# MLP and output projections as pairs of 64-row products, with ScalarE writes at the change of rows

## The chip, the cores and the metric

The kernel runs on one core of one Trainium2 chip. The metric is the time of one execution on the device, in microseconds. TensorE does the matrix products (PE in the profile; its weight loads are PEld), VectorE (DVE) and ScalarE (ACT) the elementwise work, GpSimd (POOL) products of the attention, and SyncE (SP) issues the DMAs.

## The reference

Everything is float32, with x of 2048 rows and D = 448 columns, F = 1792 hidden columns, 16 heads of 28.

```python
x = A_x
g = sigmoid((x * gate_w).sum(-1, keepdims=True))
qkv = x @ wqkv                       # q, k, v of 16 heads
# sliding window: each position attends to 8 positions, 2 apart
idx = pos[:, None] - (arange(8) * 2)[None, :]
attn = softmax(where(idx >= 0, einsum("bhsd,bhswd->bhsw", q, kg) * scale, -1e9))
a = concat_heads(einsum("bhsw,bhswd->bhsd", attn, vg)) @ wo
h = relu(x @ w1 + b1) ** 2
b = h @ w2 + b2
out = g * a + (1 - g) * b
```

## The kernel before

**Three products for one.** Each float32 operand is split into a high part, rounded to the format that TensorE takes (float32r), and a low part, the rest. A product is then high x high, high x low and low x high. ScalarE writes the high part, VectorE subtracts to get the low part (`split_full`, L108).

**The 64 odd rows.** D = 448 is three blocks of 128 rows and 64 rows. For the MLP and the output projection the odd rows are doubled: a tile of w1 holds the low part in rows 0 to 63 and the high part in rows 64 to 127 (`w17`, `split_w7`, L112), and x holds its high part twice (`x7`) and its low part twice (`x8`). Two full-row products do the work of the odd rows. `pairs` (L141) lists the nine products of the three blocks and these two: 11 for one hidden tile or one projection tile.

**Pairs in the qkv stage.** The first stage (q, k, v of four chunks of 512 rows, `qkv_first`, `qkv_two`) already works in pairs: `side_by_side` (L183) issues one product on rows 0 to 63 and one on rows 64 to 127, for two different psum tiles, so that both halves of the array work at once. A psum tile is fed by one half of the rows at a time. To change halves, `turn` (L194) lets VectorE (or, for two tiles, ScalarE) write an unused element of the psum tile; the following products wait for that write.

**The MLP.** The main loop (L821) goes through the four chunks of x in `ORDER` and the 14 tiles f of 128 hidden columns. `mlp_h` (L648) computes a hidden tile (128 x 512) with 11 products in psum bank set "m" (four buffers). `mlp_act` (L657) gives ScalarE three instructions: relu with bias in psum, the square rounded into `hh`, the square in psum; VectorE later subtracts the low part `hl`. `mlp_o` (L707) multiplies hidden tile f with w2 into four psum tiles of set "b" (128 x 448 each, one for 128 rows of x), 12 products for one f, two tiles f behind `mlp_h`. After the last f, `fin_add` (L693) has VectorE scale and add, and the result goes to DRAM.

**Attention and output projection.** GpSimd forms the products of attention beside all this (`qk_piece`, `av_piece`), VectorE reduces them. Finished rows go to DRAM and come back transposed (`wo_load`, L724), are split (`wo_split`, L742: a copy in psum, high parts by ScalarE, low parts by VectorE) and multiplied with wo (`wo_mm`, L757: 11 products for a tile of 128 rows). `wo_step` (L771) places one such tile between two hidden tiles.

**Order.** The order of the instructions on each engine is fixed when the kernel is built, by a clock of planned costs: `advance(dt)` moves it on after each group of matmuls (`MM512`, `MM448` are the planned times of one step), and runs what was put off with `at(dt, fn)`; the attention is a generator that is called by the same clock. The engines then run their queues in order, and wait for each other by semaphores.

Of the kernel before, what the change touches and what calls it, by code (L numbers as in the profile page):

```python
# [38 lines left out]
HL_DELAY = 1700.0  # L39
# [4 lines left out]
LAND_DELAY = 5000.0  # L44
KEY_DELAY = 8000.0
DEFER = 2
ORDER = (3, 0, 1, 2)
RING = 5
# [4 lines left out]
BT_BUFS = 9  # L53
# [3 lines left out]
def gated_mix_kernel(ctx: ExitStack, tc: tile.TileContext, xT, wqkv, w1, w2, wo, b1, b2, out):  # L57
# [23 lines left out]
    w17 = const.tile([P, F], F32R, name="w17")  # L81
# [3 lines left out]
    b1t = const.tile([P, 64], F32, name="b1t")[:, :NF]  # L85
    b2t = const.tile([P, D], F32, name="b2t")
    ident = const.tile([P, P], F32, name="ident")
# [4 lines left out]
    const.tile([P, 64], F32, name="pad_x")  # L92
# [6 lines left out]
    make_identity(nc, ident)  # L99
# [11 lines left out]

    def split_w7(raw, w7, soon=now):  # L112

        nc.scalar.activation(w7, raw, AF.Copy)
        soon(lambda: nc.vector.tensor_sub(w7[0:64], raw[0:64], f32(w7[0:64])))
# [24 lines left out]

    def pairs(xh, xl, x7, x8, wh, wl, w7):  # L141

        r = []
        for k in range(3):
            r += [(xh(k), wh(k)), (xh(k), wl(k)), (xl(k), wh(k))]
        r += [(x7, w7), (x8, w7)]
        return r
# [29 lines left out]
    class Acc:  # L177


        def __init__(self, tag, name, n):  # L180
            self.pt, self.n, self.todo, self.rows = ps(tag, name), n, 21, None

    def side_by_side(*todo):  # L183


        assert len(todo[0]) == len(todo[1])
        for pair in zip(*todo):
            for r, (acc, a, w) in enumerate(pair):
                rows = slice(r * 64, r * 64 + 64)
                assert acc.rows in (None, r)  # L190
                nc.tensor.matmul(acc.pt[:, :acc.n], a[rows], w[rows], start=acc.todo == 21, stop=acc.todo == 1)  # L191
                acc.todo, acc.rows = acc.todo - 1, r

    def turn(one, two):  # L194


        for acc in (one, two) if one is not two else (one,):
            if one is two:
                nc.scalar.activation(acc.pt[0:1, 511:512], ident[0:1, 1:2], AF.Copy)
            else:  # L200
                nc.vector.memset(acc.pt[0:1, 511:512], 0.0)
            acc.rows = None
# [113 lines left out]
    wo_q = []  # L316

# [32 lines left out]
    def o_store(par, s):  # L350
        nc.sync.dma_start(o_d[par, s], o_t.pop((par, s)))
        at(WO_DELAY, lambda: wo_q.append((par, s)))
# [132 lines left out]
    def w1_piece(i, dt):  # L485
# [6 lines left out]
        def part(k):  # L492
            if k < 3:
                split_full(raw[:, k, :n], w1h[:, k, sl], w1l[:, k, sl], soon)
            else:
                split_w7(raw[:, 3, :n], w17[:, sl], soon)
# [120 lines left out]
    hp = ctx.enter_context(tc.tile_pool(name="hidden", bufs=3, reuse_waits="tile"))  # L617
# [6 lines left out]
    wo7 = bw.tile([P, D], F32R, name="wo7")  # L624
# [11 lines left out]
    def x_reload(i, j):  # L636

        c = ORDER[i]
        r = (4 * i + j) % RING
        xt = (xpool if r < 4 else bw).tile([P, 2, CH], F32R, tag=f"x{r}", name=f"x{c}b_{j}")  # L640
        nc.sync.dma_start(f32(xt), x_d[c, j])
        return xt

    hs = {}
    nxt = [x_reload(1, j) for j in range(RING - 4)]
    bw.tile([P, 48], F32, name="pad_b")

    def mlp_h(x, c, f):  # L648
        pt = ps("m", f"h{c}_{f}")
        fs = slice(f * P, f * P + P)  # L650
        pr = pairs(lambda k: x.h[k], lambda k: x.l[k], x.x7, x.x8,
                   lambda k: w1h[:, k, fs], lambda k: w1l[:, k, fs], w17[:, fs])
        for i, (a, w) in enumerate(pr):
            nc.tensor.matmul(pt, w, a, start=i == 0, stop=i == len(pr) - 1)  # L654
        return pt

    def mlp_act(pt, c, f):  # L657
# [5 lines left out]
        at(HL_DELAY, lambda: nc.vector.tensor_sub(hl, pt, f32(hh)))  # L663
# [15 lines left out]

    def fin_ahead():  # L680

        for par, t, *_ in wo_cur + [w[1:] for w in wo_in]:
            fin_fetch(par, t)
# [23 lines left out]
    def mlp_o(c, *fs):  # L707
        ops = [(f, *hs.pop((c, f)), *w2hl(f)) for f in fs]
        last = fs[-1] == NF - 1
        if last:  # L710
            bts = [fin_tile(c // 2, (c % 2) * 4 + tl) for tl in range(4)]
        for tl in range(4):
            if fs[0] == 0:
                bps[tl] = ps("b", f"b{c}_{tl}")
            sl = slice(tl * P, tl * P + P)
            for f, hh, hl, wh, wl in ops:
                for i, (a, w) in enumerate(((hh, wh), (hh, wl), (hl, wh))):
                    nc.tensor.matmul(bps[tl][:, :D], a[:, sl], w, start=f == 0 and i == 0, stop=f == NF - 1 and i == 2)  # L718
        if last:
            for tl in range(4):  # L720
                par, t = c // 2, (c % 2) * 4 + tl
                fin_add(par, t, bts[tl], bps[tl][:, :D], g1t[:, par, t:t + 1])

    def wo_load(par, t):  # L724


        tag = ("ot", "k", "v", "ot")[t // 2] if par else "ot"
        raw = (bp if tag == "ot" else attp).tile([P, 8 * P], F32, tag=tag, name=f"ot{par}_{t}")
        raw = raw.rearrange("p (k t n) -> p k t n", k=4, t=2)
        src = o_d[par, t].rearrange("p c -> (p c)")  # L730

        def rows(m, n):
            return bass.AP(tensor=src.tensor, offset=src.offset + m * 32, ap=[[32, n], [32 * D, 8], [1, 32]])
        rv = raw.rearrange("p k t (q j) -> p k (t q) j", j=32)
        for k in range(3):
            nc.sync.dma_start(rv[:, k], rows(k * P, P))
        for r in range(2):
            nc.sync.dma_start(rv[r * 64:r * 64 + 64, 3], rows(3 * P, 64))
        for i in range(2):
            wo_in.append((clock["pe"] + LAND_DELAY, par, t + i, raw[:, :, i]))  # L740

    def wo_split(par, t, raw):  # L742
        oh = bp.tile([P, 3, P], F32R, tag="oh", name=f"oh{par}_{t}", bufs=2)
        ol = bp.tile([P, 3, P], F32R, tag="ol", name=f"ol{par}_{t}", bufs=2)
        o7 = bp.tile([P, P], F32R, tag="o7", name=f"o7{par}_{t}", bufs=2)
        o8 = bp.tile([P, P], F32R, tag="o8", name=f"o8{par}_{t}", bufs=2)

        pt = ps("m", f"oc{par}_{t}")
        pv = pt.rearrange("p (k n) -> p k n", k=4)
        nc.scalar.activation(oh, raw[:, 0:3], AF.Copy)  # L750
        nc.scalar.activation(pv, raw, AF.Copy)
        nc.scalar.activation(o7, raw[:, 3], AF.Copy)
        nc.vector.tensor_sub(ol, pv[:, 0:3], f32(oh))
        nc.vector.tensor_sub(o8, pv[:, 3], f32(o7))
        return (par, t, oh, ol, o7, o8)

    def wo_mm(st):  # L757
        par, t, oh, ol, o7, o8 = st
        bt = fin_tile(par, t)
        pa = ps("m", f"a{par}_{t}")  # L760
        pr = pairs(lambda k: oh[:, k], lambda k: ol[:, k], o7, o8,
                   lambda k: woh[:, k], lambda k: wol[:, k], wo7)
        for i, (a, w) in enumerate(pr):
            nc.tensor.matmul(pa[:, :D], a, w, start=i == 0, stop=i == len(pr) - 1)  # L764
        fin_add(par, t, bt, pa[:, :D], gt[:, par, t:t + 1])

    wo_loads = [0]
    wo_in = []
    wo_cur = []

    def wo_step():  # L771

        due = len(wo_cur)
        fin_ahead()
        if wo_in and clock["pe"] > wo_in[0][0]:
            wo_cur.append(wo_split(*wo_in.pop(0)[1:]))
            wo_loads[0] -= 1
        while len(wo_q) >= 2:
            (par, t), n = wo_q[0], wo_loads[0]
            if not (n == 0, True, st_["att"] == 1, n <= 4)[t // 2 if par else 0]:  # L780
                break
            del wo_q[:2]
            wo_loads[0] += 2
            at(LOAD_DELAY, lambda par=par, t=t: wo_load(par, t))
        if due:
            wo_mm(wo_cur.pop(0))
# [102 lines left out]
```

## Time and profile before

| | |
|---|---|
| median of 3 runs | 425.2 us (424.85 to 427.08) |
| profiled execution | 424.95 us |
| its span in the trace | 423.2 us |
| TensorE busy | 417.6 us (99%), 2452 matmuls |
| VectorE busy | 273.3 us (65%) |
| ScalarE busy | 185.3 us (44%) |
| GpSimd busy | 272.2 us (64%) |
| qkv stage on TensorE | about 9 to 109 us |
| MLP and projections on TensorE | about 109 to 419 us |
| granted TensorE clock | 0.999 |

How to read the lines below: a timeline row is start, duration (both us), engine, line, operation, out<-in, shapes and count; in square brackets stands the idle time before it and what ended it. A row of the chain in order of time is start, duration and what. A row of groups gives the total busy time and the mean of one instruction in ns. A row of windows gives the length of the stretch, then busy time and instructions of PE, PEld, DVE, ACT and POOL, the granted clock, the DMA share and GB/s. "h" is a hidden psum tile, "b" an MLP output tile, "a" a projection tile, "hh" and "hl" the high and low part of a hidden tile.

### The profile page before, as it was taken

The numbers are of one execution on the slowest core, as the hardware profiler recorded it, in microseconds if no ns is written. First come the engines' busy times: TensorE is split into PE (matmuls) and PEld (weight loads), VectorE is DVE, ScalarE is ACT, GpSimd is POOL, SyncE is SP. The second block draws the span as 40 slices with busy tenths as digits, with TensorE's granted clock in tenths as the row PEclk, the third lists the DMA queues.
The fourth block names the chain that finished last, engine by engine and source line by source line (L and its number), as shares of the span: only waits on it lengthen the run. The fifth ranks groups of instructions, "written<-read, shape, count | busy, mean of one in ns | idle before, by whom it ended". The sixth has DMA issues, their size and how long they took to land.

```text
span 423.2 us, 6516 instructions
## 1 busy us (share of the span) xinstructions
PE 417.6 (99%) x2452; PEld 379.5 (90%) x2452; DVE 273.3 (65%) x400; ACT 185.3 (44%) x372; POOL 272.2 (64%) x167
## 2 busy tenths in 40 slices
PE   8999999999999999999999999999999999999996
PEld 7999999999888888988888888898899888888995
DVE  4520422375499988996575699677577696692463
ACT  3642444344555543543443543534354433344750
POOL 1000000960979999999998989899979699690000
PEclk9999999999999999999999999999999999999999
DMA  7999899939624234551120779185267500237723
GB/s 234 339 338 334 231 376 286 367 102 339 227 68 188 86 137 155 198 207 50 75 83 0 237 265 255 31 237 142 71 159 246 202 24 0 88 125 148 140 87 131
DMA packets 69439, 74.10 MB, mean 175 GB/s; under 512 B 36448, under 2 KB 62496, under 8 KB 69024
## 3 DMA queue, kind: packets, MB, share of 16 engines
q1 hardware_dynamic: 69408, 73.69, 54.1%
q8 instruction: 19, 0.31, 0.3%
q14 instruction: 12, 0.10, 0.1%
HBM read 46.23 MB, written 28.25 MB: 176 GB/s over the span
## 4 chain that ended last, share of the span: by engine, by line
PE 80%; POOL 9%; DVE 6%; issue 2%; DMA 1%; ACT 0%; SPq 0%; DVEq 0%; POOLq 0%
PE h L654 24%; PE b L718 24%; PE qkv L191 23%; PE a L764 8%; POOL av L336 5%; POOL qk L329 4%; DVE w2al L110 1%; DVE wol L110 1%; PE qkv L260 1%; DMA xraw<-xT 1%; DVE o L344 1%; DVE hl L663 1%; DVE bt L694 1%; POOL lg L376 0%; DVE lg L330 0%
## 5 line engine op out<-in xcount | busy, mean ns | idle before, releaser
L329 POOL TENSOR_TENSOR qk<-q,k 128x896 f32<-128x896 f32 x64 | 138.1, 2186 | 93.5 <-DMA k<-k_d 85.6
L336 POOL TENSOR_TENSOR av<-lg,v 128x896 f32<-128x896 f32 x64 | 120.3, 1976 | 8.6 <-DMA v<-v_d 4.0
L660 ACT ACTIVATE h<-h,b1t 128x512 f32<-128x512 f32 x56 | 37.0, 661 | 146.2 <-PE h L654 146.2
L191 PE MATMUL qkv<-wqh,x 64*128 64x448 f32 (+1 forms) x528 | 90.7, 362 | 0.0
L191 PE MATMUL qkv<-wql,x 64*128 64x448 f32 (+1 forms) x264 | 75.3, 361 | 0.0
L191 PEld LDWEIGHTS qkv<-wqh,x 64*128 64x128 f32 x528 | 74.1, 184 | 0.3
L344 DVE TENSOR_REDUCE o<-av 128x112 f32<-128x896 f32 x64 | 66.9, 1066 | 3.9 <-POOL av L336 3.9
L330 DVE TENSOR_REDUCE lg<-qk 128x32 f32<-128x896 f32 x64 | 66.9, 1075 | 3.5 <-POOL qk L329 3.5
L663 DVE TENSOR_TENSOR hl<-h,hh 128x512 fp32r<-128x512 f32 x56 | 38.0, 680 | 33.0 <-ACT h L662 33.0
L210 ACT ACTIVATE st<-qkv 128x448 f32<-128x448 f32 x48 | 24.7, 544 | 48.5 <-PE qkv L191 46.3
L191 PEld LDWEIGHTS qkv<-wql,x 64*128 64x128 f32 x264 | 44.8, 184 | 0.1
L718 PE MATMUL b<-w2ah,hl 128*128 128x448 f32 x112 | 40.7, 364 | 0.3 <-DVE hl L663 0.3
L718 PE MATMUL b<-w2ah,hh 128*128 128x448 f32 x112 | 40.7, 363 | 0.0
L718 PE MATMUL b<-w2bh,hh 128*128 128x448 f32 x112 | 40.6, 363 | 0.0
L718 PE MATMUL b<-w2bh,hl 128*128 128x448 f32 x112 | 40.6, 363 | 0.0
L718 PE MATMUL b<-w2bl,hh 128*128 128x448 f32 x112 | 40.4, 361 | 0.0
L718 PE MATMUL b<-w2al,hh 128*128 128x448 f32 x112 | 40.4, 360 | 0.0
L661 ACT ACTIVATE hh<-h 128x512 fp32r<-128x512 f32 x56 | 33.6, 599 | 1.8
L662 ACT ACTIVATE h<-h 128x512 f32<-128x512 f32 x56 | 33.2, 594 | 0.0
L654 PE MATMUL h<-x1b,w1h 128*128 128x512 f32 x84 | 28.2, 390 | 0.0
L654 PE MATMUL h<-x,w1h 128*128 128x512 f32 x84 | 28.2, 390 | 0.0
L654 PE MATMUL h<-x2b,w1h 128*128 128x512 f32 x84 | 28.2, 389 | 0.0
(105 smaller groups left out, 765.9 us busy)
## 6 DMA issues: line engine op xcount, KB each, us to landing
k<-k_d SPq DMA_DIRECT2D x8, 840.0 KB, 5.1
v<-v_d SPq DMA_DIRECT2D x8, 840.0 KB, 4.6
x_d<-x SPq DMA_DIRECT2D x12, 512.0 KB, 5.1
q_d<-st SPq DMA_DIRECT2D x8, 448.0 KB, 7.7
k_d<-st SPq DMA_DIRECT2D x8, 448.0 KB, 5.0
v_d<-st SPq DMA_DIRECT2D x8, 448.0 KB, 6.3
w1raw<-w SPq DMA_DIRECT2D x4, 896.0 KB, 10.4
q<-q_d SPq DMA_DIRECT2D x8, 448.0 KB, 3.4
```

The costliest lines, as they stand in the source:

```text
L191: nc.tensor.matmul(acc.pt[:, :acc.n], a[rows], w[rows], start=acc.todo == 21, stop=acc.todo == 1)
L329: nc.gpsimd.tensor_mul(pr, q[:, s:s + 1].to_broadcast([P, W, C]), k[:, s:s + W])
L330: pending.append(lambda: nc.vector.tensor_reduce(lg[:, s], pr.rearrange("p w (h d) -> p w h d", h=HG), axis=AX.X, op=ALU.add))
L336: nc.gpsimd.tensor_mul(pr.rearrange("p (h d) w -> p w h d", h=HG), lg[:, s][:, :, :, None].to_broadcast([P, W, HG, DH]), v[:, s:s + W].rea ...
L344: nc.vector.tensor_reduce(o[:, g * C:(g + 1) * C], pr, axis=AX.X, op=ALU.add)
L654: nc.tensor.matmul(pt, w, a, start=i == 0, stop=i == len(pr) - 1)
L660: nc.scalar.activation(pt, pt, AF.Relu, bias=b1t[:, f:f + 1])
L661: nc.scalar.activation(hh, pt, AF.Square)
L662: nc.scalar.activation(pt, pt, AF.Square)
L663: at(HL_DELAY, lambda: nc.vector.tensor_sub(hl, pt, f32(hh)))
L718: nc.tensor.matmul(bps[tl][:, :D], a[:, sl], w, start=f == 0 and i == 0, stop=f == NF - 1 and i == 2)
L764: nc.tensor.matmul(pa[:, :D], a, w, start=i == 0, stop=i == len(pr) - 1)
```

## The change

The MLP's hidden products, its output products and the output projection are all issued as pairs of 64-row products, for two tiles at a time.

- The odd rows get the same three products as the others: `w17` becomes `w17h` and `w17l`, in which the even tiles f lie on rows 0 to 63 and the odd ones on rows 64 to 127; `wo7` becomes `wo7h`, `wo7l`. w1's odd rows are split in more and smaller pieces.
- Two hidden tiles f and f+1 are a couple. `h_first` issues 12 pairs (tile f on the lower half of the rows, f+1 on the upper half, with the odd rows), `h_second` the other 9 with the halves exchanged. Output tiles are taken two and two ("left" 0 and 1, "right" 2 and 3) with 6 pairs before and 6 after the exchange, and projection tiles two and two with 12 and 9.
- Between the halves stands `touch`: ScalarE copies one column of an operand of the last product onto itself (w1h for the hidden tiles, hl for the output tiles, woh for the projection). It waits for the products that read the operand, and the next products that read it wait for it.
- The order of one couple is: `h_first`; the turn of the hidden tiles; first halves of the output products of the couple before; their turn; `h_second`; relu and squares of both tiles; if there is one, the first half of a projection couple; second halves of the output products; the second half of the projection.
- For the second couple of all, the output products and their turns come after `h_second` and its relu and squares; at the end of a chunk the right tiles' first halves and turn do so.
- Projection work starts with the third chunk instead of the second, for two tiles at a time; its low parts are put off by `OL_DELAY`. Two copies into psum per tile become five ScalarE instructions per couple. In the last chunk most projection couples stand at the end.
- Buffers: four hidden buffers for three, eight for nine rows of 448, the identity tile and a pad go, x tiles are reloaded into the slots that the chunk's last products leave first.

```diff
+    def touch(ap):
+        nc.scalar.activation(ap, f32(ap), AF.Copy)
+
+    def go(todo, cost):
+        n = len(todo[0])
+        for a in range(0, n, 3):
+            side_by_side(todo[0][a:a + 3], todo[1][a:a + 3])
+            advance(min(3, n - a) * cost)
+
+    def three(acc, lh, ll, rh, rl):
+        return [(acc, lh, rh), (acc, ll, rh), (acc, lh, rl)]
...
-    def mlp_h(x, c, f):
-        pt = ps("m", f"h{c}_{f}")
...
-        for i, (a, w) in enumerate(pr):
-            nc.tensor.matmul(pt, w, a, start=i == 0, stop=i == len(pr) - 1)
-        return pt
+    def h_first(x, c, f):
+        accs = [Acc("m", f"h{c}_{f + r}", CH) for r in range(2)]
+        go([h_last(x, a, f) + h_full(x, a, f + r, (0, 1, 2)) for r, a in enumerate(accs)], MM512)
+        return accs
+
+    def h_turn(accs, f):
+        touch(w1h[:, 2].rearrange("p (f n) -> p f n", n=P)[:, f:f + 2, 0:1])
+        for a in accs:
+            a.rows = None
+
+    def h_second(x, accs, f):
+        go([h_full(x, accs[1 - r], f + 1 - r, (2, 0, 1)) for r in range(2)], MM512)
...
-        at(HL_DELAY, lambda: nc.vector.tensor_sub(hl, pt, f32(hh)))
+        at(HL_DELAY * (1 + f % 2), lambda: nc.vector.tensor_sub(hl, pt, f32(hh)))
...
+    def o_turn(c, f, tls):
+        hl = hs[c, f + 1][1].rearrange("p (t n) -> p t n", n=P)
+        touch(hl[:, tls[0]:tls[-1] + 1, 0:1])
+        for tl in tls:
+            bps[tl].rows = None
...
+    def wo_first(st):
+        _, _, accs, _, _, o7, o8 = st
+        go([wo_three(accs[r], o7, o8, wo7h, wo7l) + wo_full(st, r, (0, 1, 2)) for r in range(2)], MM448)
+        touch(woh[:, 2, 0:1])
...
+    for g in range(2 * NF):
+        i, f = g // (NF // 2), g % (NF // 2) * 2
+        c = ORDER[i]
+        pc, pf = (c, f - 2) if f else (ORDER[i - 1], NF - 2)
+        ends = f == NF - 2 and i < 3
...
+        accs = h_first(x, c, f)
...
+        h_turn(accs, f)
+        if g > 1:
+            for tls in (left, right)[:1 if ends else 2]:
+                o_part(pc, pf, False, tls)
+            o_turn(pc, pf, left if ends else both)
+        h_second(x, accs, f)
+        for r, acc in enumerate(accs):
+            mlp_act(acc.pt, c, f + r)
...
+        if g == 1:
+            for tls in (left, right):
+                o_part(pc, pf, False, tls)
+                o_turn(pc, pf, tls)
+        elif g > 1 and ends:
+            o_part(pc, pf, False, right)
+            o_turn(pc, pf, right)
+        st = at_hand() if wo_ready or last else None
+        if st:
+            wo_first(st)
...
+        if g:
+            o_all(pc, pf, True)
...
+        if st:
+            wo_second(st)
```

More of the change, by code (lines that the diff above doesn't have):

```diff
@@ L190, in side_by_side @@
                 assert acc.rows in (None, r)
-                nc.tensor.matmul(acc.pt[:, :acc.n], a[rows], w[rows], start=acc.todo == 21, stop=acc.todo == 1)
+                nc.tensor.matmul(acc.pt[:, :acc.n], a[rows], w[rows], start=acc.todo == acc.all, stop=acc.todo == 1)
                 acc.todo, acc.rows = acc.todo - 1, r
@@ L752, in wo_split @@
[L752 to L765, printed above, removed]
```

267 lines of the change are left out of this document (157 added, 110 removed).

## The prediction

> **What bounds the kernel now.** I read the page's totals first, then the chain that ended last, then that chain in order of time.
>
> ```profile
> span 423.2 us, 6516 instructions
> PE 417.6 (99%) x2452; PEld 379.5 (90%) x2452; DVE 273.3 (65%) x400; ACT 185.3 (44%) x372; POOL 272.2 (64%) x167
> PE 80%; POOL 9%; DVE 6%; issue 2%; DMA 1%; ACT 0%; SPq 0%; DVEq 0%; POOLq 0%
> ...
> 13.66 95.39 PE qkv L191 x931
> ...
> 193.10 2.49 PE h L654 x11
> 195.59 2.40 PE b L718 x12
> ...
> 269.00 2.20 PE a L764 x11
> ```
>
> TensorE works through 99% of the span and 80% of the chain is its matmuls; the shares of GpSimd and VectorE in the chain lie where TensorE is busy too. So the time is the number of TensorE steps, times what a step takes, plus the moments in which TensorE stands still. The last three rows give a full-row step: 2.49/11 = 0.2264 us for the hidden products (512 columns), 2.40/12 = 0.200 us for the MLP's output products and 2.20/11 = 0.200 us for the output projection (448 columns). The qkv stage (L191) already runs as pairs of 64-row products, so it shows what a pair costs.
>
> **Steps that go.** Today a hidden tile is 11 products and so is a projection tile: nine for three full row blocks, two for the 64 odd rows doubled. As pairs, two tiles take 12 pairs, then 9 with the halves exchanged: 21 pairs where 22 full-row products stood. There are 28 such couples of hidden tiles and 8 of projection tiles: 28 x 0.2264 + 8 x 0.200 = 7.94 us go. The MLP's output products keep their count (24 full-row products become 24 pairs for two hidden tiles). This is all that the change can gain on TensorE.
>
> **What a pair costs.**
>
> ```profile
> 16.31 0.43 PE L191 MATMUL qkv<-wql,x 64*128 64x448 f32 x2
> 16.91 0.43 PE L191 MATMUL qkv<-wql,x 64*128 64x448 f32 x2
> ...
> 90.58 0.36 PE L191 MATMUL qkv<-wql,x 64*128 64x448 f32 x1
> 91.20 0.36 PE L191 MATMUL qkv<-wql,x 64*128 64x448 f32 x1
> ...
> 15.00:105.00 90.00, 90.00 (x891) 89.55 (x889) 33.02 (x87) 38.77 (x93) 17.57 (x8) 1.00 0.88 297
> ```
>
> A low-part product comes once in three pairs. At 16 us it returns after 0.60 us, a pair every 0.200 us, exactly a full-row step. At 90 us, where the two halves have drifted apart, it returns after 0.62 us: 0.207 us. Over the stage the window gives 90.00/(891/2) = 0.2020 us (it counts the instructions on its edges too, so it is a floor), and the chain row 95.39/(931/2) = 0.2049 us. I take the middle, 0.2035 us: 3.5 ns more than a full-row step, with 0 and 7 ns as ends. No 512-column pair runs today; with the same 3.5 ns it takes 0.230 us. After the change there are 28 x (21 + 24) + 8 x 21 = 1428 pairs, so this costs 1428 x 3.5 ns = 5.0 us (0 to 10.0). Net gain on TensorE: 2.9 us, between 7.9 and minus 2.1.
>
> **The turns.** When a psum tile changes its rows, ScalarE copies one column of an operand onto itself; it waits for the products that read it, and the next products wait for it. That write stands in ScalarE's queue behind everything issued before. Its price is the time that it is late, less the TensorE work placed between.
>
> ```profile
> 111.58 0.39 PE L654 MATMUL h<-x,w1h 128*128 128x512 f32 x1
> 111.78 0.66 ACT L660 ACTIVATE h<-h,b1t 128x512 f32<-128x512 f32 x1 [1.68 <-PE h L654]
> 112.47 0.60 ACT L661 ACTIVATE hh<-h 128x512 fp32r<-128x512 f32 x1
> 112.97 0.59 ACT L662 ACTIVATE h<-h 128x512 f32<-128x512 f32 x1
> ...
> 118.03 0.60 ACT L662 ACTIVATE h<-h 128x512 f32<-128x512 f32 x1
> 118.55 0.41 ACT L368 ACTIVATE lg<-lg 128x256 f32<-128x256 f32 x1
> 118.86 0.56 ACT L109 ACTIVATE w2ah<-w2raw 128x448 fp32r<-128x448 f32 x1
> ...
> L218 ACT ACTIVATE zg<-qkv 128x1 f32<-128x1 f32 x16 | 2.6, 166 | 0.0
> ...
> 185.16 0.67 DVE L663 TENSOR_TENSOR hl<-h,hh 128x512 fp32r<-128x512 f32 x1
> ...
> 185.88 0.47 PE L718 MATMUL b<-w2ah,hl 128*128 128x448 f32 x1 [0.25 <-DVE hl L663]
> ...
> 186.19 0.37 PE L718 MATMUL b<-w2ah,hh 128*128 128x448 f32 x1
> ```
>
> ScalarE starts 0.20 us after the matmul step has passed (111.58 to 111.78). Relu and the two squares of one tile follow at 0.69, 0.50 and 0.52 us (112.47 - 111.78, 112.97 - 112.47, 118.55 - 118.03); the six of two tiles in a row take 1.71 + 1.19 + 0.59 = 3.49 us. Other ScalarE work in between: a weight split about 0.47 us (0.56 less the overlap of 0.1), an exponential 0.31. The turn's own write is one to four columns: L218's 0.17 us is the nearest. Restart of TensorE after a wait: 185.16 + 0.67 to 185.88 is 0.05 us, and the next step comes after 0.31 instead of 0.20: 0.16 in all.
>
> In the steady part the turn costs nothing. The hidden tiles' turn has the 12 pairs of the output products in front of it (12 x 0.2035 = 2.44 us), the output products' turn the 9 pairs of the second hidden half (2.07 us), the projection's turn 12 output pairs. ScalarE's six instructions begin when the second hidden half ends and have then 12 output pairs and 12 hidden pairs (2.44 + 2.76 = 5.20 us) before the next turn is asked for. If that cover were gone, each turn would cost 0.20 + 0.17 + 0.16 = 0.53 us.
>
> At five places the written order leaves too little:
> - First couple: nothing lies between its halves: 0.53 us.
> - Second couple, hidden turn: again nothing between, and the write stands behind the first couple's six instructions and a split: 0.20 + 3.49 + 0.47 + 0.17 + 0.16 = 4.49 us after the first couple's end, less its own 12 pairs (2.76): 1.73 us.
> - Second couple, output turn: behind the second couple's six and a split, 4.49 us after its end; 12 output pairs cover 2.44: 2.05 us.
> - The end of each of the first three chunks of x: the right tiles' turn is issued after the last couple's six instructions: 0.20 + 3.49 + 0.17 + 0.16 = 4.02 us after the second half's end, against 12 pairs (right first halves, left second halves) of 2.44: 1.58 us, three times. A weight split stands in the first (0.47), an exponential in the third (0.31): 5.5 us.
>
> Together 0.53 + 1.73 + 2.05 + 5.5 = 9.8 us. Behind each late write nothing else of ScalarE's queue is urgent.
>
> **The low parts.** The lag between a hidden tile and its use shrinks. Today two hidden tiles and two lots of output products (2 x 2.49 + 2 x 2.40 = 9.78 us) lie between; afterwards 5.20 us do, plus five pairs (1.0 us) for the second tile, whose low part is ready at the earliest 0.20 + 3.49 + 0.69 = 4.4 us after the couple's end. The margin falls to 1.8 us, and VectorE is full in this stretch:
>
> ```profile
> 118.21 1.08 DVE L330 TENSOR_REDUCE lg<-qk 128x32 f32<-128x896 f32 x1
> ...
> 118.46 6.33 POOL L329 TENSOR_TENSOR qk<-q,k 128x896 f32<-128x896 f32 x3
> 119.20 6.08 DVE L110 TENSOR_TENSOR w2al<-w2raw,w2ah 128x448 fp32r<-128x448 f32 x1
> 125.20 0.68 DVE L663 TENSOR_TENSOR hl<-h,hh 128x512 fp32r<-128x512 f32 x1
> ...
> 130.00:140.00 10.00, 10.00 (x49) 8.80 (x48) 10.00 (x13) 4.29 (x9) 10.00 (x7) 1.00 0.22 81
> ...
> L110 DVE TENSOR_TENSOR w2bl<-w2raw,w2bh 128x448 fp32r<-128x448 f32 x7 | 9.1, 1295 | 0.0
> ```
>
> The w2al subtraction waited through three GpSimd products, and the hidden low part behind it began 125.20 - 118.55 = 6.65 us after its square; today 9.78 us hide that. Afterwards the same subtraction is ready near 118.5 us, where GpSimd is between two instructions. If it gets in there, the low part behind it is in time and the cost is 0. Two reductions (1.08 us each by the first row) and the low part (0.69) follow it: ready at 118.5 + 0.6 + 2.15 + 0.69 = 121.9 us, when TensorE asks for it. If it waits as it did, until GpSimd stands still (two more products of 6.33/3 = 2.11 us, 122.7 us), the low part ends at 126.1 and, less the output turn's wait that runs meanwhile, 2.0 us are added. The seven w2bl subtractions take 1.30 us on the mean, so they waited for less than one product: I take 0 and keep 2.0 for the range; the later couples come out just in time at such durations. The Trainium skill (SBUF — State Buffer, section "SBUF: two separate sides") says that VectorE and GpSimd hold their shared port for one whole instruction and the other blocks until then: by that rule the term is 0, by the w2al row 2.0; that row, through three instructions, does not agree with the rule.
>
> **The end.** Today the output adds follow one by one, and one of 0.68 us lies behind the last matmul:
>
> ```profile
> 418.85 0.37 PE L718 MATMUL b<-w2bh,hl 128*128 128x448 f32 x1
> 419.25 0.68 DVE L694 SCALAR_TENSOR_TENSOR bt<-b,zg,bt 128x448 f32<-128x448 f32 x1 [0.52 <-PE b L718]
> ```
>
> Afterwards both tiles of the last couple end with the same pair, so two adds follow: 0.6 us more. Smaller edits are hidden: 12 more ScalarE and VectorE splits of the odd w1 rows beside qkv pairs (ScalarE 38.77 of 90 us busy), fewer projection copies, the loads of x, which keep over 6 us.
>
> **Sum.** The profiled execution took 424.95 us (span 423.2 and 1.75 around it), 0.25 under the median of 425.2. 424.95 - 7.94 + 5.0 + 9.8 + 0.6 = 432.4 us.
>
> **The rivals.**
> - Pairs keep the full-row pace of 16 us (for: the couples start in step after each wait; against: the stage's mean): 424.95 - 7.94 + 9.8 + 0.6 = 427.4 us.
> - Pairs run at 0.207 us as at 90 us: 1428 x 7 ns = 10.0 us instead of 5.0: 437.4 us.
> - VectorE becomes the bound in the first chunk: low parts 6.65 us late against 1.8 us of margin add up to 4.9 us: 437.3 us. For it VectorE's full window; against it that TensorE itself is later there by the turns.
> - The other side: a 512-column pair is shorter than a full-row product, because the two halves hide each other's start, which at 448 columns no row shows (against it). It decides from 7.5 ns under 0.2264 us: 588 hidden pairs x 7.5 ns = 4.4 us bring 427.4 to 423.0; at 13 ns it is 7.6 us and 419.8 us.
> - The halves do not run side by side when they stream the same tile of x: 1428 steps of 0.2 us more, over 700 us. The qkv pairs share their x tile and do overlap; 1 in 100.
>
> **How the numbers follow.** Forecast 0.44, full pace 0.24, slow pairs 0.11, VectorE 0.12, other side 0.08, not side by side 0.01. About 0.5% (2.1 us) is what a measurement of this kernel tells from no change: 423.1 to 427.3 us. Faster holds the other side and a sliver of the full-pace case: 0.10. The full-pace case straddles the upper edge and gives most of "same": 0.16. The rest, 0.74, is slower. The range goes from 424 (full pace, turns a third cheaper) to 438 us (either slow case); outside lie the other side and the case of 1 in 100, and a combination of the two slow cases.
>
> **What would show it.** In the changed profile: 21 pairs of the hidden products in 4.7 to 4.9 us of work; TensorE waiting for ScalarE at the self-copy's line five or six times, near 112, 117, 123 us and at each chunk's end for 1.5 to 2.1 us; ScalarE's relu and squares standing before the late write; two adds after the last matmul. It is wrong if TensorE shows no such idle time, if the pairs stand far from 0.2035 and 0.230 us, or if waits for low parts exceed those for ScalarE.

## The result and the profile after

The changed kernel takes 437.77 us in the median (434.57 to 438.8, 4 runs) against 425.44 us for the kernel before on the same chip: 1.0271 times as long, 95% interval 1.0208 to 1.0333. The profiled execution took 438.8 us, its span is 437.0 us; the times below are of this execution.

First the page of the changed kernel: span, busy times, granted clock in 40 slices, chain.

```profile
span 437.0 us, 9342 instructions
PE 416.8 (95%) x3844; PEld 376.8 (86%) x3844; DVE 268.0 (61%) x405; ACT 196.1 (45%) x445; POOL 271.1 (62%) x165
...
PEclk9999999999969999998999999999999999999999
...
PE 81%; ACT 7%; DVE 4%; DMA 4%; issue 2%; POOL 1%; SPq 1%; DVEq 0%; POOLq 0%
```

TensorE is busy for as long as before (416.8 and 417.6 us) in a span that is 13.8 us longer; ScalarE has gone from 0% to 7% of the chain; and the clock row has two dips that the row of before has not. That TensorE is no less busy, although 7.9 us of steps are gone, is in part a sign of the dips: a pair of 448 columns there counts as busy for 0.37 us instead of 0.20, 3.5 us in all. The rest are slow restarts and short waits that count as busy too. In the run with all three edits below, which has no dip, TensorE is busy for 411.8 us.

The chain in order of time (start, duration, what; here a pair is two instructions) gives the pace and the end:

```profile
149.37 2.40 PE b L178 x24
151.77 2.72 PE h L178 x24
...
425.26 4.20 PE a L178 x42
429.46 1.20 PE b L178 x12
430.66 1.82 PE a L178 x18
432.49 0.03 issue
432.51 0.68 DVE bt L712
```

2.40/12 = 0.200 us for a pair of 448 columns, 2.72/12 = 0.2267 us for one of 512, 4.20/21 = 0.200 us in the projection: the full-row steps were 0.200, 0.2264 and 0.200 us. Behind the last product come 437.0 - 432.48 = 4.5 us; before it were 423.2 - 419.23 = 4.0.

Then the timeline of TensorE, those rows that carry idle time in brackets (all with at least 0.3 us):

```profile
111.90 0.50 PE L178 MATMUL h<-x,w1h 64*128 64x512 f32 x2 [0.30 <-ACT w1h L646]
118.38 0.50 PE L178 MATMUL h<-x,w1h 64*128 64x512 f32 x2 [1.43 <-ACT w1h L646]
126.03 0.74 PE L178 MATMUL b<-w2ah,hl 64*128 64x448 f32 x2 [4.27 <-DVE hl L686]
165.56 0.47 PE L178 MATMUL b<-w2bh,hl 64*128 64x448 f32 x2 [0.52 <-DVE hl L686]
181.88 0.47 PE L178 MATMUL b<-w2bh,hl 64*128 64x448 f32 x2 [1.74 <-ACT hl L646]
199.37 0.74 PE L178 MATMUL b<-w2ah,hl 64*128 64x448 f32 x2 [1.89 <-DVE hl L686]
254.73 0.48 PE L178 MATMUL b<-w2bh,hl 64*128 64x448 f32 x2 [1.28 <-ACT hl L646]
271.22 0.47 PE L178 MATMUL b<-w2ah,hl 64*128 64x448 f32 x2 [0.91 <-DVE hl L686]
342.34 0.47 PE L178 MATMUL b<-w2bh,hl 64*128 64x448 f32 x2 [1.58 <-ACT hl L646]
```

There are two kinds: five stops for ScalarE's turns (L646) and four for VectorE's low parts (L686). Each stop also restarts slowly: the 14 products after 165.5 us take 1.68 us in the chain where 1.40 would do, 0.28 us more. At 126.03 and 199.37 us a pair takes 0.74 instead of 0.47 us: there the clock is down, as the windows show (granted clock is the third number from the end).

```profile
122.00:124.00 2.00, 0.00 (x0) 0.00 (x0) 2.00 (x2) 1.97 (x5) 0.90 (x1) 0.94 0.00 0
124.00:126.00 2.00, 0.00 (x0) 0.00 (x0) 2.00 (x4) 0.74 (x2) 1.54 (x1) 0.50 0.00 0
126.00:128.00 2.00, 1.97 (x10) 1.81 (x12) 1.88 (x4) 0.21 (x1) 1.45 (x3) 0.50 0.23 30
130.00:132.00 2.00, 2.00 (x20) 1.86 (x18) 2.00 (x2) 0.00 (x0) 2.00 (x2) 0.85 0.97 360
```

Two microseconds into the stop the granted clock falls to 0.50 and comes back near 130.6 us. The chain has 6.19 us there for 37 products, 2.5 us over their 3.7; near 199 us it is 2.98 us for 14.

Why the low part at 126 us was late, in the timelines of GpSimd and VectorE:

```profile
118.12 0.66 POOL L353 TENSOR_TENSOR lg<-lg,mx 128x256 f32<-128x256 f32 x1
118.71 4.20 POOL L317 TENSOR_TENSOR qk<-q,k 128x896 f32<-128x896 f32 x2
...
118.26 5.12 DVE L109 TENSOR_TENSOR w2al<-w2raw,w2ah 128x448 fp32r<-128x448 f32 x1 [1.48 <-ACT w2ah L108]
123.31 2.07 DVE L318 TENSOR_REDUCE lg<-qk 128x32 f32<-128x896 f32 x2
125.30 0.68 DVE L686 TENSOR_TENSOR hl<-h,hh 128x512 fp32r<-128x512 f32 x1
```

The weight subtraction lasts as long as GpSimd runs without a break (118.12 to 122.9 us). Two reductions and the hidden low part stand behind it.

And the start of the second chunk run in the chain:

```profile
194.05 0.59 ACT bt L698
194.64 0.02 issue
194.66 0.60 DVE bt L712
195.26 0.00 issue
195.26 0.68 DVE bt L712
195.94 0.60 DVE hl L686
196.54 0.99 DVE o L332
197.53 1.18 DVE bt L712 x2
198.71 0.61 DVE hl L686
```

The output adds of the chunk that has ended (L712) wait for copies of the bias that ScalarE makes behind its six relu and square instructions (L698), and the second low part stands behind the adds. The adds also hold the psum tiles that the new chunk's output products write, as the view of waits says for the weight loads (us in total, times, longest):

```profile
PEld b L178 <- DVE bt L712: 1.2, 4, 0.4
```

**Where 13.8 us come from.** Steps that went: -7.9. Turns: idle 6.33, five restarts 1.40, together 7.7. Low parts: idle 4.27 + 0.52 + 1.89 + 0.91 and one of 0.12 us near 145.6, 7.7, with five restarts 9.1. Two more gaps before each late chunk start (0.30 + 0.39 us, twice), where products wait for psum that the adds have not read: 1.4. Half clock: 6.19 - 3.70 - 0.28 = 2.2 and 2.98 - 1.40 - 0.28 = 1.3, together 3.5. End: 0.5. Less the 0.4 us that the one stop of the kernel before cost: 13.9 us.

### The profile page after: what moved, and what is told of

Its sections match the earlier page's. It is cut to its first block, busy times and chain, and to the rows that moved or that the text cites. A ratio compares the mean times of both kernels' runs of the same rounds, so it can differ in the third digit from the quotient of the medians.

```text
span 437.0 us, 9342 instructions
## 1 busy us (share of the span) xinstructions
PE 416.8 (95%) x3844; PEld 376.8 (86%) x3844; DVE 268.0 (61%) x405; ACT 196.1 (45%) x445; POOL 271.1 (62%) x165
## 4 chain that ended last, share of the span: by engine, by line
PE 81%; ACT 7%; DVE 4%; DMA 4%; issue 2%; POOL 1%; SPq 1%; DVEq 0%; POOLq 0%
PE b L178 27%; PE h L178 26%; PE qkv L178 19%; PE a L178 8%; ACT h L683 2%; DMA k<-k_d 2%; ACT hh L684 2%; ACT h L685 2%; POOL qk L317 1%; DVE bt L712 1%; PE qkv L247 1%; DMA xraw<-xT 1%; DVE hl L686 1%; DVE lg L318 1%; DMA w2raw<-w 1%
## 5 line engine op out<-in xcount | busy, mean ns | idle before, releaser
L178 PE MATMUL qkv<-wql,x 64*128 64x448 f32 (+1 forms) x264 | 75.1, 362 | 0.0
L686 DVE TENSOR_TENSOR hl<-h,hh 128x512 fp32r<-128x512 f32 x56 | 38.4, 686 | 59.3 <-ACT h L685 59.2
L683 ACT ACTIVATE h<-h,zg 128x512 f32<-128x512 f32 x56 | 36.7, 656 | 50.9 <-PE h L178 50.9
L178 PE MATMUL b<-w2ah,hl 64*128 64x448 f32 x224 | 43.4, 383 | 7.2 <-DVE hl L686 7.1
L178 PE MATMUL b<-w2bh,hl 64*128 64x448 f32 x224 | 40.7, 364 | 5.1 <-ACT hl L646 4.6
L178 PE MATMUL b<-w2ah,hh 64*128 64x448 f32 x224 | 43.1, 371 | 0.2
L178 PE MATMUL b<-w2al,hh 64*128 64x448 f32 x224 | 42.6, 369 | 0.0
L178 PE MATMUL b<-w2bh,hh 64*128 64x448 f32 x224 | 40.7, 359 | 0.0
L178 PE MATMUL b<-w2bl,hh 64*128 64x448 f32 x224 | 40.6, 358 | 0.0
L646 ACT ACTIVATE hl<-hl 128x4 fp32r<-128x4 f32 (+1 forms) x33 | 6.8, 207 | 60.7 <-PE b L178 60.7
L178 PEld LDWEIGHTS b<-w2ah,hl 64*128 64x128 f32 x224 | 22.4, 194 | 10.9 <-DVE hl L686 9.5
L178 PE MATMUL h<-x,w1h 64*128 64x512 f32 x168 | 29.2, 390 | 1.7 <-ACT w1h L646 1.7
```

Of the source, the lines that this page charges most:

```text
L646: nc.scalar.activation(ap, f32(ap), AF.Copy)
L683: nc.scalar.activation(pt, pt, AF.Relu, bias=b1t[:, f:f + 1])
L686: at(HL_DELAY * (1 + f % 2), lambda: nc.vector.tensor_sub(hl, pt, f32(hh)))
```

## The experiments

### The three causes, one by one and together

**Turns ahead of the six instructions, at the end of the chunks.**

```diff
         h_second(x, accs, f)
-        for r, acc in enumerate(accs):
-            mlp_act(acc.pt, c, f + r)
         if ends:
...
+            o_part(pc, pf, False, right)
+            o_turn(pc, pf, right)
+        for r, acc in enumerate(accs):
+            mlp_act(acc.pt, c, f + r)
...
-        elif g > 1 and ends:
-            o_part(pc, pf, False, right)
-            o_turn(pc, pf, right)
```

> At the end of the first three chunks the right tiles' first output products and their turn are now issued ahead of the six relu and square instructions; TensorE's own order is the same. Theory (the turn is late only because of what stands before it in ScalarE's queue): the three stops of TensorE at 180, 253 and 341 us (1.74, 1.28 and 1.58 us, with the slow restart 1.91 + 1.46 + 1.75 = 5.1 us) go, 437.8 becomes about 432.7 us. Rival (the time comes back): the six instructions now start about 1.4 us later, so the low parts of the same couple come later by as much and TensorE stops for them at the next couple instead, near 185, 258 and 346 us: 437 us or no gain. Second rival: the next chunk's x, which had the stop to land in, becomes the next late thing: about half of the gain stays, 435 us.

429.31 us (428.9 to 432.82; 1.0112 of the kernel before, 1.0064 to 1.0159). The profiled execution is the one of 432.82 us, span 431.0, 6.0 us less than the changed kernel. In its chain the place of the first of the three stops reads:

```profile
176.20 2.04 PE h L178 x18
178.24 3.60 PE b L178 x36
181.84 2.72 PE h L178 x24
```

36 products without a gap; the other two stops are gone as well. No new stop for a low part or for x has come, so both rivals fall. The rest of the 6.0 us goes with the dip of the clock near 199 us, which did not come this time, although the stop there is as long as before (1.89 us). The stop at 126 us is still there in this execution (4.17 us, with its dip). The three other executions took 428.9 to 429.6 us, at a granted clock of 0.996 to 1.000 where this one has 0.992; they have no trace, but the next run shows what they may lack.

**Bias copies two couples earlier.**

```diff
             o_turn(pc, pf, left if ends else both)
+        if f >= NF - 4:
+            for tl in left if f == NF - 4 else right:
+                par, t = c // 2, (c % 2) * 4 + tl
+                if (par, t) not in fin and (par, t) not in ahead:
+                    ahead[par, t] = fin_begin(par, t)
         h_second(x, accs, f)
```

> The four copies of the output bias at the end of the first and second chunk run (chunks whose output tiles have no partial sum yet) are given to ScalarE two couples ahead of the add that needs them, not behind the six relu and square instructions. Theory (the stops at the chunks' starts, 195 to 199 and 268 to 271 us, come from the four output adds that wait for these copies on VectorE and hold up the psum tiles and the second low part): 0.30 + 0.39 + 2.07 and 0.30 + 0.39 + 1.07 us go, and the 1.4 us of half clock behind the first of them: 437.8 becomes about 431.9 us. Rival (VectorE is simply full there, the reductions and the low parts in a row take as long in any order): only the psum waits go, 1.4 us, 436.4 us.

428.06 us (427.71 to 428.8; 1.0065, 1.0043 to 1.0087), span 426.3. The stops at the chunks' starts and their psum gaps are gone, as the theory has it, and so is the dip there. But the span fell by 10.7 us, not 5.9: the stop at 126 us is gone too, which this edit does not touch. GpSimd and VectorE there:

```profile
118.42 0.64 POOL L353 TENSOR_TENSOR lg<-lg,mx 128x256 f32<-128x256 f32 x1
119.00 6.66 POOL L317 TENSOR_TENSOR qk<-q,k 128x896 f32<-128x896 f32 x3
...
118.62 0.91 DVE L109 TENSOR_TENSOR w2al<-w2raw,w2ah 128x448 fp32r<-128x448 f32 x1 [1.48 <-ACT w2ah L108]
```

The same subtraction, again issued while GpSimd's small one runs, got in behind it this time and took 0.91 us instead of 5.12. The two kernels issue the same instructions up to here, so this stop probably comes and goes from one execution to the next, and is one source of the changed kernel's spread (434.57 to 438.8 us) and of the gap of 3.2 us and more between the executions of the run before. No kernel has two traces that show it with and without the stop. Where it is missing, TensorE runs into the second couple's output turn instead: a stop of 1.38 us for ScalarE at 125 us.

**The low part of w2's row 4 later.**

```diff
-        at(5000.0, lambda: split_full(raw, *w2hl(f), soon))
+        at(5000.0, lambda: split_full(raw, *w2hl(f), soon if f > 4 else lambda fn: at(8000.0, fn)))
```

> The low part of the weight row 4 of w2 (needed near 138 us) is given to VectorE 8 us after its high part, not 1.5 us: behind the low parts of the second and third hidden couple's first tiles. Theory (that subtraction waits 5.1 us for GpSimd and holds up the hidden low part behind it): the stop of TensorE at 121.8 to 126.0 us goes (4.4 us with its restart), and with it the half clock from 124 to 130 us (2.2 us): 437.8 becomes about 431.2 us, granted clock 1.0 from 120 to 132 us. Rival A (the hidden low part itself waits for GpSimd's products, as the weight's did): the stop stays, within 1 us, 437 us. Rival B (the wait only moves: the row's subtraction, or that of row 5, meets GpSimd's products later and holds up the next low parts): a stop of 2 to 4 us between 128 and 140 us, 434 to 437 us. If the clock drops without a stop, it isn't tied to the stop: 433.5 us.

433.07 us (432.86 to 434.31; 1.019, 1.0155 to 1.0226), span 431.2, 5.8 us less. The clock reads 1.00 through this stretch, and the stop is another one:

```profile
125.13 0.47 PE L178 MATMUL b<-w2ah,hl 64*128 64x448 f32 x2 [1.74 <-ACT hl L646]
```

The low part of the second tile is done at 119.9 us, while GpSimd is busy: a subtraction with one operand in psum does not wait for it, so rival A falls, and B too. What I had left out is the turn behind the stop: 6.7 us went with the low part, 2.0 came back as a wait for ScalarE, the hidden turn before it waits 0.3 us longer (1.70 us), and the second dip (1.3 us) failed to come here also, again behind a stop as long as before (1.90 us).

**All three.**

> The three edits together. Theory (the causes add): 437.8 - 5.1 - 5.9 - 6.7 = 420.1 us, 1.2% under the kernel before: what is left are the steps that went (7.9 us) less the hidden turns of the first two couples (2.2 us). Rival (behind the stops TensorE was not the only late engine; VectorE with GpSimd bounds the first chunk): stops of 0.5 us and more come up at other couples, 425 to 430 us.

424.83 us (424.41 to 426.06, 10 runs; 0.9999, 0.9985 to 1.0012). 14.0 us of span have gone, and the kernel is as fast as before. The three causes explain that it was slower, but they do not add up to the 17.7 us of the forecast: the result is 4.7 us above it, near the rival's 425 us. TensorE still stops in the first two couples (0.30, 1.42, 1.73 us; the last is the output turn that the low part had hidden), for low parts at 141, 160 and 258 us (0.12, 0.50, 0.75 us) and once for x (0.29 us). That is 5.1 us of idle time and 2.0 of restarts, and the end keeps its 0.5: what the missing steps bring is spent.

### The clock by itself

To the kernel with the three edits, near 201 us, 13 needless copies were added ahead of one turn; then the same with 18 products that nobody reads in the stop.

```diff
+        if g == 9:
+            touch(w1h[:, 2].rearrange("p (f n) -> p f n", n=P)[:, f:f + 2, 0:1])
+            for _ in range(13):
+                nc.scalar.activation(b2t, b2t, AF.Copy)
         h_turn(accs, f)
```

```diff
+        if g == 9:
+            idle = ps("m", "idle")
+            for _ in range(18):
+                nc.tensor.matmul(idle, w1l[:, 0, 0:P], x.h[0], start=True, stop=True)
         h_second(x, accs, f)
```

> The three edits, and in one hidden couple near 215 us ScalarE makes 13 needless copies (about 0.5 us each) ahead of the hidden turn, so that TensorE stops for 13 x 0.5 - 2.4 = 4.1 us once; nothing else is changed. Theory (a stop of 4 us makes the granted clock fall, as at 122 us of the changed kernel): 0.5 in the granted clock from about 2 us into the stop, for 3.4 or 6.8 us, and the products behind it at half pace: 424.8 + 4.3 + 1 to 2.4 = 430.1 to 431.5 us. Rival (the fall of the clock at 122 us had another cause than the stop): clock 1.0 throughout, 429.1 us.

> The same stop near 215 us, but TensorE has 18 products of 512 columns to do in it whose result nobody reads (18 x 0.2264 = 4.1 us). Theory (it is the idleness that brings the clock down): clock 1.0 throughout, 424.8 + 4.3 = 429.1 us, 1 to 2.4 us under the run with the bare stop. Rival (the clock falls for another reason): the same time as the bare stop.

432.46 us (2 runs) with the bare stop and 430.97 us (2 runs) with the filled one. The copies took 7.87 us, 0.6 each, not 0.5: the stop is 5.77 us, and both times lie above their forecasts. In the filled run 1.47 us of idle time is left. The windows of the first:

```profile
206.00:208.00 2.00, 0.94 (x4) 0.83 (x6) 0.00 (x0) 1.08 (x4) 0.00 (x0) 0.62 0.00 0
208.00:210.00 2.00, 2.00 (x12) 1.52 (x10) 0.00 (x0) 0.00 (x0) 0.00 (x0) 0.52 0.00 0
210.00:212.00 2.00, 2.00 (x22) 1.81 (x22) 0.00 (x0) 1.21 (x3) 0.00 (x0) 1.00 0.00 0
```

and of the second:

```profile
206.00:208.00 2.00, 0.76 (x6) 0.67 (x8) 0.00 (x0) 1.26 (x4) 0.00 (x0) 1.00 0.00 0
208.00:210.00 2.00, 2.00 (x20) 1.76 (x19) 0.00 (x0) 0.37 (x1) 0.00 (x0) 1.00 0.00 0
```

The products after the stop start at 207.06 and 207.24 us, but only the bare stop brings the clock down: 0.62 and 0.52 in two windows of 2 us are 1.52 + 1.92 = 3.4 us at half clock. 432.46 - 430.97 = 1.5 us (1.2 to 1.8 between single executions) is the price of this dip alone. That it follows from the idleness is shown: the filled run differs by the 18 products and has no dip.

### Towards a faster version

Five runs moved what was left. The first puts ScalarE's turns in the first couples earlier:

```diff
-        at(HL_DELAY * (1 + f % 2), lambda: nc.vector.tensor_sub(hl, pt, f32(hh)))
+        at(due or HL_DELAY * (1 + f % 2), lambda: nc.vector.tensor_sub(hl, pt, f32(hh)))
...
         h_turn(accs, f)
+        if g == 1:
+            mlp_act(*held, HL_DELAY)
...
+        if g == 1:
+            o_part(pc, pf, False, left)
+            o_part(pc, pf, False, right)
+            o_turn(pc, pf, both)
         for r, acc in enumerate(accs):
-            mlp_act(acc.pt, c, f + r)
+            if g or not r:
+                mlp_act(acc.pt, c, f + r)
+        held = (accs[1].pt, c, f + 1)
```

> The three edits, and in the first two hidden couples ScalarE's writes moved forward: the second couple's hidden turn goes ahead of the second tile of the first couple, its output turn ahead of the second couple's own six instructions. TensorE's order is the same. With the three edits alone TensorE still stopped there for 1.42 us (116.9 to 118.5 us) and 1.72 us (123.2 to 125.0 us), 1.58 and 1.89 us with the restarts. Theory (each turn costs what stands before it in ScalarE's queue): the hidden turn falls to the bare 0.5 to 0.6 us of the first couple, the output turn to 0.2 or nothing: 424.8 - 1.0 - 1.7 = 422.1 us. Rival (GpSimd and VectorE set the pace of the first chunk): ScalarE's later relu and squares make the low parts late instead, a stop for VectorE of 1 us or more between 120 and 135 us: 424 to 425 us.

424.01 us (0.9983, 0.9969 to 0.9996). The output turn fell from 1.73 to 0.30 us, the hidden turn from 1.42 to 0.81, as that theory says; but row 4's subtraction, in another place now, waited 5.21 us for GpSimd again, and low parts were late by 0.31 and 0.89 us at 129 and 140 us. Both the theory and its rival hold in part.

The second also places the second low part of each couple earlier:

```diff
-        at(due or HL_DELAY * (1 + f % 2), lambda: nc.vector.tensor_sub(hl, pt, f32(hh)))
+        at(due or HL_DELAY + f % 2 * 1000.0, lambda: nc.vector.tensor_sub(hl, pt, f32(hh)))
```

> As the run with the first couples' turns moved forward, and the second tile's low part of every couple is placed 2.8 us, not 3.6 us, after its products in VectorE's order, that is ahead of one or two reductions or weight splits that stood before it. Theory (the stops of 0.3 and 0.7 us at 140 and 160 us come from the order on VectorE alone): both go, 0.9 us, 421.2 us against 422.1 us. Rival (VectorE waits in order for the square and the reductions behind it make GpSimd late): no change or 0.5 us slower.

424.88 us (0.9994, 0.9972 to 1.0017): no gain. The stop at 140 us went, but others came at 149 and 189 us (0.43, 1.25 us), and that at 159 us grew from 0.51 to 0.90. The rival was nearer.

The third starts from the first again and puts the weight rows' low parts, of w2 and of wo, behind the second hidden low part of a couple:

```diff
-        at(5000.0, lambda: split_full(raw, *w2hl(f), soon if f > 4 else lambda fn: at(8000.0, fn)))
+        at(5000.0 if f > 4 else 9000.0, lambda: split_full(raw, *w2hl(f), behind.append))
...
-            at(5000.0, lambda: split_full(raw, woh[:, k], wol[:, k], soon))
+            at(5000.0, lambda: split_full(raw, woh[:, k], wol[:, k], behind.append))
...
+        def low():
+            nc.vector.tensor_sub(hl, pt, f32(hh))
+            while f % 2 and behind:
+                behind.pop(0)()
...
-        nc.vector.reciprocal(gt[:, par], e)
+        at(4000.0, lambda: nc.vector.reciprocal(gt[:, par], e))
```

> As the run with the first couples' turns moved forward, and on VectorE the low parts of all w2 and wo weight rows now stand behind the second hidden low part of a couple, the reciprocals of the gates 4 us later, and the high part of w2's row 4 is taken 4 us later, out of the way of the second couple's hidden turn. Theory (what is left of the stops in the first chunk, 0.97 + 0.47 + 1.05 + 0.68 us, stands in the queues ahead of the turn and of the low parts): the stops at 129, 139 and 160 us fall to 0.1 us or less, that at 117 us to 0.55 us: 424.0 - 2.4 = 421.6 us, 0.8% under the kernel before. Rival (VectorE, 63% busy, and GpSimd are the bound there in any order): the stops move and the time stays at 424 us, as with the run that had the low parts placed sooner.

424.33 us (0.9974, 0.9959 to 0.9989). The named stops fell as forecast (0.30 us at 117, 0.03 and 0.05 at 128 and 139, none at 160 us), but two wo subtractions took 4.60 us from 177.5 us on, and the start of the next chunk run stopped for 1.66 us. The time is the rival's (424), not the theory's (421.6).

The fourth takes the edit of the wo rows back:

```diff
-            at(5000.0, lambda: split_full(raw, woh[:, k], wol[:, k], behind.append))
+            at(5000.0, lambda: split_full(raw, woh[:, k], wol[:, k], soon))
```

> As the run before it, but the low parts of the wo rows stand where they stood (1.5 us behind their high parts); those of w2, the gates' reciprocals and row 4 stay moved. Theory (in the run before, two wo subtractions put behind the low parts near 177 us waited 4.5 us for GpSimd and made the adds and low parts at the chunk's start late, a stop of 1.67 us at 189 us, and a wo split waited for its DMA at 173 us): these two stops go, 424.3 - 2.1 = 422.2 us. Rival (a subtraction of two SBUF operands meets GpSimd wherever it is put): another stop of 1 us or more between 160 and 195 us, 423.5 to 424.5 us.

424.18 us (0.9968, 0.9955 to 0.9982). The stop at 189 us is gone, but the wait for a turn at 174 us has grown from 0.20 to 0.97 us, and that for a low part at 259 us from 0.68 to 0.91; in the median nothing was gained, and the time lies in the rival's range.

In the last, the right tiles' adds stand behind the next low part:

```diff
+            if tls[0] and c != ORDER[3]:
+                at(1300.0, lambda: adds(pts))
+            else:
+                adds(pts)
```

> The same, and the output adds of the two right tiles of a chunk stand behind the second hidden low part of the next chunk's first couple, not ahead of it. Theory (at 257 us VectorE does adds, low part, adds, low part in a row, and TensorE needs the second low part before the right tiles' psum): the stop of 0.7 to 0.9 us at 258 us shrinks to 0.3 us or less, 0.5 us under the kernel without this edit, 421.7 us. Rival (the right psum tiles are then what comes late): no change, within 0.2 us.

423.51 us (421.54 to 427.85, 12 runs) against 424.92 us: 0.9972, 0.9951 to 0.9992. The stop at 259 us is gone; VectorE there:

```profile
255.36 1.28 DVE L689 TENSOR_TENSOR hl<-h,hh 128x512 fp32r<-128x512 f32 x2
256.56 1.26 DVE L718 SCALAR_TENSOR_TENSOR bt<-b,zg,bt 128x448 f32<-128x448 f32 x2
```

The two low parts now follow each other. Two weight loads wait for psum instead (0.40 and 0.41 us), which costs TensorE some 0.7 us where the late low part had cost 0.91 and a restart: the theory holds, and its rival in part. This version is 0.3% faster than the kernel before (0.1 to 0.5%); of the 7.9 us of steps that went, 1.4 arrive.

## Why the prediction was right, and where it was not

It said 432.4 us, 424 to 438, and slower with 0.74. The kernel is slower, and 437.77 us lies just inside the range; but the sum is made of other terms than forecast, and errors of both signs met in it. That the number fell inside the range is luck in good part: the upper end stood for slow pairs, which there are not, or for a VectorE that bounds the first chunk, which holds in part; late adds and the clock, in no forecast, filled the rest.

- **Steps that go, 7.94 us: right.** The instruction counts agree: 28 x 22 + 56 x 12 + 16 x 11 = 1464 full-row products became 1428 pairs (2452 - 1464 = 3844 - 2 x 1428), and a pair has the full-row pace.
- **What a pair costs, 5.0 us: wrong, it is 0 (0.3 ns at 512 columns).** The step that failed was to take 0.2035 us from the qkv stage. The chain's row counts 931 products where the stage has 936 (4 chunks x 4 tiles x 3 x 21, less the 72 that the first tiles do on full rows) and holds the stage's edges, but 95.39/468 = 0.2038 us is still above 0.200. The mean mixes stretches at 0.200 us, as at 16 us, with slower ones such as that at 90 us (0.207), where the halves had drifted apart. In the changed kernel a turn comes after 6 to 12 pairs, and the pace stays at the 0.200 us of the row at 16 us. That the turns keep the halves in step is my reading of this; no run varied it. The rival "full pace" was right on this point, and its 427.4 us would have been the forecast but for the terms below. The rivals of slow and of shorter pairs and of halves that do not overlap are out.
- **Turns, 9.8 us: right in each size.** Bare turn 0.30 + 0.28 = 0.58 us (0.53 forecast); second couple 1.43 + 0.28 = 1.71 (1.73); its output turn, seen where the low part was in time, 1.74 + 0.28 = 2.02 (2.05; 1.38 + 0.28 = 1.66 in the run with the bias copies earlier); the chunk ends 2.02, 1.56 and 1.86 (2.05, 1.58, 1.89). The run with the turns ahead of the six instructions shows that the place in ScalarE's queue was the reason. In the profiled execution the output turn hid behind a later low part, so 7.7 us show. In the steady part there is none, as forecast.
- **Low parts, taken as 0: the step that failed, 9.1 us.** The text worked out both cases: the subtraction gets in, or the low part ends at 126.1 us. It ended at 125.98. What I took for the likelier case is the rarer one in the traces: of four profiled executions with such a subtraction in this place (the kernel before, the changed one and the first two edits), three show 5.0 to 6.1 us and one 0.91. My own sign for "wrong" is met: waits for low parts (7.7 us) exceed those for ScalarE (6.3). The rule of the Trainium skill that was weighed there (SBUF — State Buffer, section "SBUF: two separate sides") would give the 0 only if VectorE got its turn after one GpSimd instruction; at 5.12 us through three it did not, at 0.91 us it did.
- **Left out: the chunks' starts.** That the output adds wait for bias copies at the end of ScalarE's queue, and that psum and the second low part wait for the adds, is the same mechanism as the late turns, and the queue was in the code; I followed only the turns' instructions. 1.89 + 0.91 us of stops, 0.56 of restarts and 1.38 of psum gaps are 4.7 us, and one of the two dips stands behind them.
- **Left out: the clock.** The granted clock of before was 0.999 in the mean, and I did not ask what a stop of TensorE does to it. That profile had a hint: the last product ends at 419.2 us, and the window from 422 to 423 us reads 0.85, so the clock falls some 3.5 us into the idle end. The two dips cost 3.5 us.
- **End, 0.6 us: right** (0.5).
- **VectorE as the bound in the first chunk,** a rival at 437.3 us, named the right engine and nearly the right time. Only one of its late low parts was of the size that it gave, and moving one subtraction took it away; the later runs, where stops of 0.3 to 1.3 us moved rather than went, are on its side again.

From forecast to profiled execution: 432.4 - 5.0 (pairs) - 2.1 (the output turn that hid) + 9.1 (low parts) + 1.4 (psum behind the adds) + 3.5 (clock) - 0.4 (own stop of before) - 0.1 (end) = 438.8 us.

## What to carry to other kernels

A change that removes work from the bounding engine also removes the cover under which the other engines' queues ran late: follow every instruction behind the lengthened group on each queue (here turns, bias copies, adds and low parts alike), not only the one that the change adds. Take the pace of a step from neighbouring rows of a steady stretch that is built like the new code, not from a stage's mean. And price a stop of TensorE above its own length, with the restart and, if it is long or one of several close together, the half clock that can follow it.

## What the hardware showed

The dips of the clock come in steps of one length: 198.88 to 202.3 us in the changed kernel and 206.5 to 209.9 us in the run with the bare stop are 3.4 us, 123.76 to 130.6 us is twice that, and the two dips of the changed kernel begin 75.1 us, 22 such steps, apart. Laying this grid over each trace from its own changes of clock, the windows before a dip in the changed kernel are these two:

```profile
120.34:123.76 3.42, 1.42 (x14) 0.94 (x10) 3.42 (x2) 2.91 (x6) 2.56 (x2) 1.00 0.00 0
195.46:198.88 3.42, 1.89 (x12) 0.91 (x10) 3.42 (x6) 0.94 (x3) 1.27 (x1) 1.00 0.36 134
```

and two that no dip followed are, in the run with the turns first and in that with the bare stop:

```profile
196.27:199.69 3.42, 1.86 (x18) 1.72 (x20) 3.42 (x6) 0.15 (x1) 2.73 (x2) 1.00 0.66 219
199.65:203.07 3.42, 1.64 (x18) 1.19 (x14) 1.29 (x2) 3.26 (x6) 3.42 (x3) 1.00 0.70 228
```

14 and 12 products in a window (a full one, from 216 us on, counts 35) are followed by the half clock, 18 are not. Nor are 16 in the run with the bias copies earlier (175.83 to 179.25 us on the grid of its one fall, at 425.0 us), so in these traces the limit lies between 14 and 16. The modelled busy time does not sort them: 1.89 us was followed by a dip, 1.64 us was not. So the same stop of 1.9 us brought the clock down in the changed kernel and not in two other runs: in these traces it goes with how the stop lies on the grid and how thin the products around it are. No run varied the count by itself. The Trainium skill (TensorE: Matmul & The Clock Gate, section "What's actually happening") has a free-running window of 3413 ns; the 3.4 us here agree. It asks for no gap above some 3 us (section "Why this matters for your kernels"); here a stop of 1.89 us in a thin window was enough.

A subtraction of two SBUF operands by VectorE (w2al, wol) can wait out GpSimd's products, through as many as follow without a break (5.12 us through three instructions, 4.60 us for two subtractions), but in one execution it got in after the first (0.91 us). One with an operand in psum (hl, 0.68 us at 119.2 us of the run with row 4 later) passes beside them.
